# Putting the last four residual-token tiles of a routed MLP behind a run-time branch

## The chip, the cores and the metric

One core of one Trainium2 chip runs the whole program in one launch. Five engines work side by side, each through its own instruction list: PE (matrix products), DVE (vector), ACT (scalar, activation functions), POOL (here mostly the issue of gathers and scatters) and SP (here only the issue of DMAs). Engines wait for each other on semaphores. The metric is the device time of one execution in microseconds (us).

## The reference

An attention without softmax, then a mixture of experts with one expert per token, then a dense MLP, all in float32. Cut to what matters:

```
out  = u * (relu(z z^T / S)^2 v)                 # 8 batches, S = 3072, D = 256
x    = out as 24576 tokens of 256
e    = argmax of the cosine logits of x, per token, over 8 experts
y[t] = gate[t] * (relu(x[t] w1[e]) w2[e])        # hidden width 1024
res  = elu(y w_in) w_out                         # hidden width 2048
```

Which expert a token goes to is known only once the attention is done, so the counts of the experts are numbers on the chip, while the program is fixed.

## The kernel before

The program is unrolled: a list of *steps* is built first (lines 1323 to 1370), and one loop at the end (lines 1555 to 1571) emits for each step its PE work, its DVE and ACT work with a lag of one step, and the second matrix product with a lag of two (LAG). Tasks such as loads and gathers are hung on a step number with `at`. That emission order is the order on every engine: nothing reorders it later.

The steps come in units:

- Attention: 48 chunks of 512 tokens (to 1.9 ms of the run).
- **A**, 41 tiles of 512 tokens that all belong to one expert: 4 steps, `ab_h` and `a_acc`, 96 matmuls of 512 columns.
- **B**, 21 tiles of up to 256 *residual* tokens (what an expert has left after its full tiles): 2 steps, `ab_h` and `b_acc`, 96 matmuls of 256 columns. Its rows are gathered through the id list, and its results are scattered into a dense table `dn` (3584 rows) and their ids into `dnid`.
- **M**, the dense MLP of an A tile: 8 steps of 24 matmuls of 512 columns (`m_h` and `m_acc`).
- **D**, the dense MLP of the 3584 residual tokens in `dn`: 7 tiles of 512, each like an M.

The order is six A with their M, then triples A, B, M as long as there are B tiles, then pairs A, M, then the seven D.

The 21 is the most that the counts can make necessary (`NB`, line 43). A plan computed by DVE (`plan2_ops`, line 857) makes `G`, the number of 256-row tiles of each expert's residue, its running sum `cG`, and `tl`, the last sum less one. A tile with a number above `tl` takes the indices of tile `tl` again, and its scatter indices are raised by 1.0e6, beyond the bound of the scatter:

```
lambda: ts(keep("tl", [128, 1]), K["cG"][:, E - 1:E], -1.0, ALU.add),
lambda: ts(k2("tq"), K["jt"][:, :J], K["tl"], ALU.min),
lambda: tt(k2("ov"), K["jt"][:, :J], h["tq"], ALU.is_gt),
```

Buffers: working tiles come from 45 slots of 4 KB per partition (tag "g"); `pss` and `psa` are PSUM tiles, two each. A matmul that writes a `pss` buffer waits for the engines that last read it.

Of the kernel before, what the change touches and what calls it, by code (L numbers as in the profile page):

```python
# [7 lines left out]
F32 = mybir.dt.float32  # L8
F32R = mybir.dt.float32r
BF16 = mybir.dt.bfloat16  # L10
I32 = mybir.dt.int32
# [17 lines left out]
def attn_moe_mlp(ctx, tc, zT, zK, uT, v, emb, embT, tau, wp, w_in, w_out, out):  # L29
    nc = tc.nc  # L30
    B, DZ, S = zT.shape
    D = uT.shape[1]
# [8 lines left out]
    NA = ceil_div(N - E * 511, 512)  # L41
    NR = N - 512 * NA
    NB = (NR + E * 255) // 256
    ND = NR // 512
    NA1 = 6
    MAXT = 8
    assert D == 256 and DZ == 64 and E == 8 and NR % 512 == 0 and NR <= 14 * 256
# [6 lines left out]
    XW = D + 64  # L54
# [8 lines left out]
    mir = {(b, c, k): dr.tile([128, 2048], F32, name="mir")  # L63
           for b in range(B) for c in range(NC) for k in range(c + 1, NC)}

    def slot(name, dt=F32, shape=(2, 512)):
        return sb.tile([128] + list(shape), dt, name=name, tag="g", bufs=NSLOT)

    def rslot(name):
        return slot(name, F32R)  # L70

    def wide(name, shape):
        return sb.tile([128] + shape, F32, name=name, tag="wide", bufs=NWIDE)

    def t_sm():
        return sb.tile([128, MAXT * E], F32, name="sm", tag="sm", bufs=11)

    def t_ps():
        return ps.tile([128, 2, 512], F32, name="pss", tag="s", bufs=2)

    def t_acc():
        return ps.tile([128, 2, 512], F32, name="psa", tag="acc", bufs=2)

    def const(shape, dt, name):
# [7 lines left out]
    def ts(o, a, s1, op0, s2=None, op1=None):  # L92
        if op1 is None:
            vec.tensor_scalar(out=o, in0=a, scalar1=s1, scalar2=None, op0=op0)
        else:
            vec.tensor_scalar(out=o, in0=a, scalar1=s1, scalar2=s2, op0=op0, op1=op1)
# [37 lines left out]
    def at(n, fn, s=0):  # L134
        tasks[n][s].append(fn)
# [722 lines left out]
    def plan2_ops():  # L858
        NA2 = NA - NA1
        J = NB  # L860
        h = {}

        def start_():
            arena["t"], arena["o"] = [], 0
            tt(keep("c2", [128, E]), K["run"], K["eoff"], ALU.subtract)

        def k3(n):
            h[n] = keep(n + "B", [128, J, E])
            return h[n]

        def k2(n, w=None):
            h[n] = keep(n + "B", [128, J] if w is None else [128, J, w])
            return h[n]

        def dot_(name, src, ind):
            return [lambda: tt(k3("x" + name), h[ind], bj(K[src], J), ALU.mult),
                    lambda: red(k2(name), h["x" + name], ALU.add)]
        ops = [start_] + full_ops("c2", "F2")
        ops += [lambda: tt(K["F2"], K["F2"], K["takena"], ALU.subtract)]
        ops += cum_ops("F2", "cF2") + tile_plan_ops(NA2, "F2", "cF2", "b", "takena")  # L880
        ops += [
            lambda: tt(keep("tk2", [128, E]), K["F2"], K["cF2"], ALU.subtract),
            lambda: ts(K["tk2"], K["tk2"], float(NA2), ALU.add, 0.0, ALU.max),
            lambda: tt(K["tk2"], K["tk2"], K["F2"], ALU.min),
            lambda: tt(K["tk2"], K["tk2"], K["takena"], ALU.add),
            lambda: stt(keep("r", [128, E]), K["tk2"], -512.0, K["c2"], ALU.mult, ALU.add),
            lambda: tt(keep("gt", [128, E, 14]), be_(K["r"], 14),
                       K["mr"].unsqueeze(1).broadcast_to([128, E, 14]), ALU.is_gt),
            lambda: red(keep("G", [128, E]), K["gt"], ALU.add)]
        ops += cum_ops("G", "cG")  # L890
        ops += [
            lambda: ts(keep("tl", [128, 1]), K["cG"][:, E - 1:E], -1.0, ALU.add),
            lambda: ts(k2("tq"), K["jt"][:, :J], K["tl"], ALU.min),
            lambda: tt(k3("cmp"), b2(h["tq"], J, E), bj(K["cG"], J), ALU.is_ge),
            lambda: red(k2("e"), h["cmp"], ALU.add),
            lambda: ts(k2("w"), h["e"], 128.0, ALU.mult, K["pcol"], ALU.add),
            lambda: vec.tensor_copy(keep("wiB", [128, J], I32), h["w"]),
            lambda: onehot(k3("oh"), h["cmp"])]
        ops += dot_("g", "G", "cmp") + dot_("p", "r", "cmp") + dot_("k", "tk2", "oh") + dot_("r", "r", "oh")
        ops += [  # L900
            lambda: tt(h["g"], h["tq"], h["g"], ALU.subtract),
            lambda: stt(h["r"], h["g"], -256.0, h["r"], ALU.mult, ALU.add),
            lambda: ts(h["e"], h["e"], float(N), ALU.mult),
            lambda: stt(h["e"], h["k"], 512.0, h["e"], ALU.mult, ALU.add),
            lambda: stt(h["e"], h["g"], 256.0, h["e"], ALU.mult, ALU.add),
            lambda: stt(h["p"], h["g"], 256.0, h["p"], ALU.mult, ALU.add),
            lambda: ts(k2("cl"), h["r"], -1.0, ALU.add),
            lambda: tt(k2("ixf", 2), tpj(J, 2), b2(h["cl"], J, 2), ALU.min),
            lambda: tt(h["ixf"], h["ixf"], b2(h["e"], J, 2), ALU.add),
            lambda: vec.tensor_copy(keep("ixB", [128, J, 2], I32), h["ixf"]),  # L910
            lambda: tt(k2("ov"), K["jt"][:, :J], h["tq"], ALU.is_gt),
            lambda: tt(k2("od", 2), tpj(J, 2), b2(h["r"], J, 2), ALU.is_ge),
            lambda: tt(h["od"], h["od"], b2(h["ov"], J, 2), ALU.add),
            lambda: ts(h["od"], h["od"], 1.0e6, ALU.mult),
            lambda: tt(h["od"], h["od"], b2(h["p"], J, 2), ALU.add),
            lambda: tt(h["od"], h["od"], tpj(J, 2), ALU.add),
            lambda: vec.tensor_copy(keep("dpB", [128, J, 2], I32), h["od"])]

        return ops + [arena.clear]
# [43 lines left out]
    def rows_ops(key):  # L963
        kind, j = key
        nt = 4 if kind == "A" else 2

        def idx(t):
            if kind == "A":
                return K["ixa"][:, j, t:t + 1] if j < NA1 else K["ixb"][:, j - NA1, t:t + 1]
            return K["ixB"][:, j, t:t + 1]  # L970
        h = {}

        def gi(t):
            def fn():
                if t == 0:
                    IDS[key] = sb.tile([128, 4], I32, name="ids", tag="ids", bufs=8)
                    h["x"] = wide("rows", [4, XW])
                gather(IDS[key][:, t:t + 1], tok[:, :], idx(t), E * N - 1)
            return fn

        def gx(t):
            def fn():
                gather(h["x"][:, t], xr[:, :], IDS[key][:, t:t + 1], N - 1)
            return fn
        row = (j if kind == "A" else NA + j) * 512
        rows = xg[row:row + nt * 128, :]

        def gate(t):
            def fn():
                x = h["x"][:, t]  # L990
                ts(x[:, :D], x[:, :D], x[:, D:D + 1], ALU.mult)
            return fn

        def put():
            sp.dma_start(rows.rearrange("(t p) d -> p t d", p=128), h["x"][:, :nt, :D])

        def get():
            h["t"] = slot("xt", F32, (16, 2, 32))
            for i in range(4):
                sp.dma_start(h["t"][i * 32:(i + 1) * 32, :nt * 4].rearrange("p b a c -> p b (a c)"),  # L1000
                             rows.rearrange("(b r) d -> r b d", r=32)[:, :, i * 64:(i + 1) * 64])
        return [gi(t) for t in range(nt)] + [gx(t) for t in range(nt)], [gate(t) for t in range(nt)], put, get, h
# [40 lines left out]
    def ab_d(key, i):  # L1043
        lo = rslot("lo")
        stt(lo, PS.pop((key, i)), 0.0, f(HL[key, i][0]), ALU.max, ALU.subtract)
        HL[key, i][1] = lo
# [293 lines left out]
        units += [("A", j), ("M", j - 1)]  # L1340
    units += [("M", NA1 - 1)]
    j, t = NA1, 0
    while j < NA and t < NB:
        units += [("A", j), ("B", t), ("M", j)]
        j += 1
        t += 1
    if j < NA:
        units += [("A", j)]
        j += 1
        while j < NA:  # L1350
            units += [("A", j), ("M", j - 1)]
            j += 1
        units += [("M", NA - 1)]
    elif t < NB:
        last = units.pop()
        while t < NB:
            units += [("B", t)]
            t += 1
        units.append(last)
    units += [("D", i) for i in range(ND)]  # L1360
    mf = {"h": m_h, "g": m_g, "d1": m_d, "d2": m_d2, "d3": m_hi, "d4": m_lo, "acc": m_acc}
    lf = dict(mf, h=l_h, acc=l_acc)
# [131 lines left out]
    for un in units:  # L1494
# [47 lines left out]
        if k in "MD" and un != units[-1]:  # L1542
# [4 lines left out]
            at(w + 2, get)  # L1547
            spread(sc, w + 4, w + 6)

    def emit(n, k):  # L1550
        if 0 <= n < len(steps):
            steps[n][0].get(k, none)(*steps[n][1])

    for n in range(len(steps) + LAG):
        emit(n, "h")
        emit(n - 1, "d1")
        one_task(n)
        emit(n - 1, "d2")
        one_task(n)
        emit(n - 1, "d3")  # L1560
        one_task(n)
        emit(n - 1, "d4")
        for fn in pre.pop(n, ()):
            fn()
        emit(n - LAG, "acc")
        emit(n, "g")
        run_tasks(n)
# [42 lines left out]
```

## Time and profile before

| | us |
|---|---|
| median of 3 runs | 5202.31 |
| lowest, highest | 5199.91, 5210.75 |
| profiled execution | 5196.12 |
| its span, first to last instruction | 5194.3 |
| PE busy in it | 5159.3 (99%) |
| DVE busy in it | 4146.7 (80%) |
| ACT busy in it | 3540.4 (68%) |
| POOL busy in it | 1424.0 (27%) |

A matmul's start is recorded and its end is modelled, so how fast PE goes is read from the distance of starts. In the steady state a 512-column matmul starts 0.227 us after the one ahead of it, and a 256-column one 0.120 us.

### The profile page before, as it was taken

What the parts mean: (1) busy time and instruction counts of PE and PEld (TensorE: products, weight loads), DVE (VectorE), ACT (ScalarE), POOL (GpSimd) and SP (SyncE); (2) the same over time, 40 slices, a digit from 0 to 9 for tenths busy, and PEclk for the clock granted to TensorE, in tenths of its full rate; (3) what the DMA queues carried; (4) which work ended last, traced back from release to release, by engine and by line L of the source; (5) the groups of instructions that cost most, each with busy time, mean ns of one, the idle gap of its engine ahead of it and who ended that gap; (6) DMA issues with size and microseconds to landing.
All of it is one profiled execution on the core that took longest, in us unless ns stands there. A gap on an engine that the chain in (4) does not pass through costs nothing. (4 is left out here: it accounts for less than half of the span.)

```text
span 5194.3 us, 67824 instructions
## 1 busy us (share of the span) xinstructions
PE 5159.3 (99%) x23792; PEld 4301.4 (83%) x23792; DVE 4146.7 (80%) x5425; ACT 3540.4 (68%) x4196; POOL 1424.0 (27%) x1207
## 2 busy tenths in 40 slices
PE   9999999999999999999999999999999999999998
PEld 7888888888888878888888888888888888888887
DVE  8888888888888877887777777787787777777887
ACT  8676777767676855676666666666666666666776
POOL 0111111111111133334444444444444333331011
PEclk9999999999999999999999999999999999999999
DMA  7988888797969694323433433434433333231221
GB/s 234 232 214 213 212 199 222 201 223 201 222 183 233 186 233 135 86 75 112 120 107 104 124 102 108 127 102 115 115 105 101 83 84 84 84 82 50 46 48 37
DMA packets 720983, 720.15 MB, mean 139 GB/s; under 512 B 422460, under 2 KB 628543, under 8 KB 705280
## 3 DMA queue, kind: packets, MB, share of 16 engines
q1 hardware_dynamic: 643584, 502.17, 38.4%
q0 software_dynamic: 77056, 213.63, 13.5%
q8 instruction: 188, 3.08, 0.3%
q14 instruction: 155, 1.27, 0.1%
HBM read 450.95 MB, written 254.14 MB: 136 GB/s over the span
## 5 line engine op out<-in xcount | busy, mean ns | idle before, releaser
L111 PE MATMUL psa<-hi,v 128*128 128x512 f32 x4608 | 1143.3, 390 | 0.2 <-DVE hi L510 0.2
L111 PEld LDWEIGHTS psa<-hi,v 128*128 128x128 f32 x4608 | 862.6, 188 | 181.9 <-DVE hi L510 2.2
L111 PE MATMUL pss<-x2h,wi 128*128 128x512 f32 x2624 | 808.7, 389 | 0.0
L111 PE MATMUL psa<-hi,wo 128*128 128x512 f32 x3008 | 743.0, 389 | 0.0
L100 DVE SCALAR_TENSOR_TENSOR y<-e,y 128x1024 f32<-128x1024 f32 x384 | 467.4, 1217 | 301.7 <-ACT e L1164 274.3
L111 PEld LDWEIGHTS psa<-hi,wo 128*128 128x128 f32 x3008 | 564.4, 188 | 117.0
L1110 ACT ACTIVATE e<-pss 128x1024 f32<-128x1024 f32 x376 | 386.4, 1028 | 396.1 <-PE pss L111 355.0
L111 PE MATMUL psa<-lo,v 128*128 128x512 f32 x2304 | 618.0, 390 | 8.1 <-DVE lo L90 7.2
L1036 ACT ACTIVATE hi<-pss 128x1024 fp32r<-128x1024 f32 x206 | 211.9, 1029 | 588.2 <-PE pss L111 556.0
L426 ACT ACTIVATE r<-pss 128x1024 f32<-128x1024 f32 x336 | 344.8, 1026 | 362.9 <-PE pss L111 344.6
L727 POOL DMA_INDIRECT tok<-idt,pi x192 | 236.6, 1233 | 1278.4 <-DMA tok<-idt,pi 771.8
L111 PEld LDWEIGHTS pss<-x2h,wi 128*128 128x128 f32 x2624 | 489.8, 188 | 99.4
L111 PEld LDWEIGHTS psa<-lo,v 128*128 128x128 f32 x2304 | 431.5, 188 | 103.1 <-DVE lo L90 12.0
L111 PE MATMUL pss<-x2l,wi 128*128 128x512 f32 x1312 | 510.4, 389 | 0.0
L90 DVE TENSOR_TENSOR lo<-r,hi 128x1024 fp32r<-128x1024 f32 x336 | 408.4, 1215 | 124.6 <-ACT hi L108 122.3
L90 DVE TENSOR_TENSOR y<-r,y 128x1024 f32<-128x1024 f32 x384 | 470.5, 1225 | 34.6 <-DVE y L100 2.3
L930 POOL DMA_INDIRECT out<-o,ids x192 | 238.5, 1242 | 944.2 <-DMA o<-orow 485.2
L90 DVE TENSOR_TENSOR lo<-y,hi 128x1024 fp32r<-128x1024 f32 x384 | 470.7, 1226 | 20.4
L1164 ACT ACTIVATE e<-e 128x1024 f32<-128x1024 f32 x384 | 407.8, 1062 | 12.2
L1163 ACT ACTIVATE y<-e 128x1024 f32<-128x1024 f32 x384 | 407.2, 1060 | 9.5
L111 PE MATMUL psa<-hi,w 128*128 128x512 f32 x1312 | 404.9, 390 | 0.0
L111 PE MATMUL pss<-xh,w 128*128 128x512 f32 x1312 | 404.3, 389 | 0.3 <-DVE lo L100 0.2
(184 smaller groups left out, 9566.9 us busy)
## 6 DMA issues: line engine op xcount, KB each, us to landing
mir<-mt SPq DMA_DIRECT2D x120, 1024.0 KB
mr<-mir SPq DMA_DIRECT2D x960, 128.0 KB
vs<-v SPq DMA_DIRECT2D x48, 512.0 KB
u<-uT SPq DMA_DIRECT2D x48, 512.0 KB
xr<-xt SPq DMA_DIRECT2D x192, 128.0 KB
x<-xr SPq DMA_DIRECT2D x48, 512.0 KB
orow<-xt SPq DMA_DIRECT2D x188, 128.0 KB
o<-orow SPq DMA_DIRECT2D x47, 512.0 KB
```

Of the source, the lines that this page charges most:

```text
L90: vec.tensor_tensor(out=o, in0=a, in1=b, op=op)
L100: vec.scalar_tensor_tensor(out=o, in0=a, scalar=s, in1=b, op0=op0, op1=op1)
L111: pe.matmul(o, lhsT=l, rhs=r, start=start, stop=stop, skip_group_check=True)
L426: act.activation(out=r, in_=p, func=AF.Relu, scale=1.0 / S)
L727: pool.indirect_dma_start(out=tok[:, :], out_offset=bass.IndirectOffsetOnAxis(ap=h["pi"][:, t:t + 1], axis=0), in_=K["idt"][:, gt:gt + 1], ...
L930: pool.indirect_dma_start(out=dst, out_offset=bass.IndirectOffsetOnAxis(ap=idx, axis=0), in_=src, in_offset=None, bounds_check=bound, oob_ ...
L1036: act.activation(out=hi, in_=p, func=AF.Relu)
L1110: act.activation(out=e, in_=p, func=AF.Relu, scale=-1.0)
L1163: act.activation(out=y, in_=e, func=AF.Tanh, scale=0.5)
L1164: act.activation(out=e, in_=e, func=AF.Exp, scale=-1.0)
```

## The change

The units now hold 17 of the 21 B tiles (`NBS`): there are 17 triples and then pairs. The other four stand, one after the other, in a block between the last M and the first D. At the block every engine reads one number and either goes through the block or jumps over it. The number is `tl`, copied to an integer (`taken_tiles`) in the plan and loaded into a register of each engine three steps ahead of the block; the block is entered if it is at least 17, that is, if more than 17 tiles hold rows. Inside the block, tiles are taken in turn from a small set allotted for it (17 of the "g" slots, both `pss`, one `psa`).

```diff
+    NBS = NB - 4
...
     def slot(name, dt=F32, shape=(2, 512)):
+        if fixed:
...
+            t = again("gr" if dt == F32R else "g")[:, :w]
...
             lambda: ts(keep("tl", [128, 1]), K["cG"][:, E - 1:E], -1.0, ALU.add),
+            lambda: vec.tensor_copy(keep("taken_tiles", [128, 1], I32), K["tl"]),
...
-    while j < NA and t < NB:
+    while t < NBS:
         units += [("A", j), ("B", t), ("M", j)]
...
+    def load_count():
+        count["v"] = nc.values_load(K["taken_tiles"][0:1, 0:1], min_val=0, max_val=NB)
+
+    def rest_tiles():
+        with tc.If(count["v"] >= NBS):
+            mine = {"g": [slot("rest", F32, (1024,)) for _ in range(5)],
+                    "gr": [slot("restr", F32R, (1024,)) for _ in range(12)], "wide": [wide("rows", [4, XW])],
+                    "s": [t_ps() for _ in range(2)], "acc": [t_acc()],
+                    "ids": [sb.tile([128, 4], I32, name="ids", tag="ids", bufs=8)]}
+            fixed.update(mine)
+            for t in range(NBS, NB):
...
+            fixed.clear()
+
+    n_rest = start["D", 0]
+    at(n_rest - 3, load_count)
...
     for n in range(len(steps) + LAG):
+        if n == n_rest:
+            rest_tiles()
         emit(n, "h")
```

On PE, before, the first D tile's matmuls (`pss<-xh,wi`) stand right behind the last M tile's (`psa<-lo,wo`):

```order
L111 MATMUL psa<-lo,wo 128x512 [waits DVE_49]
L111 MATMUL psa<-lo,wo 128x512 x3
L111 MATMUL pss<-xh,wi 128x512 [waits PE_49,Activation_49]
L111 MATMUL pss<-xh,wi 128x512
L111 MATMUL pss<-xl,wi 128x512 [waits DVE_49]
```

Now a compare-and-branch stands between them, then the block (its matmuls read and write `restr`, `pss`, `psa`), and then the end of the block, whose second branch is the way for those that jumped:

```order
L134 MATMUL psa<-lo,wo 128x512 [waits DVE_49]
L134 MATMUL psa<-lo,wo 128x512 x3
L1574 COMPARE_AND_BRANCH
L134 MATMUL pss<-restr 128x256 [waits PE_49,Activation_49]
L134 MATMUL pss<-restr 128x256 [waits DVE_49] x2
...
L1574 UNCONDITIONAL_BRANCH
L1574 UNCONDITIONAL_BRANCH [waits PE_49]
L134 MATMUL pss<-xh,wi 128x512 [waits DVE_49,PE_49,Activation_49]
L134 MATMUL pss<-xh,wi 128x512
L134 MATMUL pss<-xl,wi 128x512
```

The jump waits for PE's own last matmul, and the first D matmul, which waited for PE and ACT, now waits for DVE too.

On DVE, now, the same gate stands behind the `lo` of the last M tile's seventh step, and DVE's last work in the block reads `pss`:

```order
L1203 CAST hi<-y 128x1024 [waits DVE_49]
L113 TENSOR_TENSOR lo<-y,hi 128x1024 [waits DVE_49,PE_49]
L1574 COMPARE_AND_BRANCH
L117 TENSOR_SCALAR rows<-rows 128x256 [waits DMASW2_49]
...
L123 SCALAR_TENSOR_TENSOR restr<-pss,restr 128x1024 [waits Activation_49] x2
L1574 UNCONDITIONAL_BRANCH
L1574 UNCONDITIONAL_BRANCH [waits DVE_49]
L123 SCALAR_TENSOR_TENSOR y<-e,y 128x1024 [waits PE_49,Activation_49]
```

Before, that `lo` and the next `y` stood side by side. ACT has the gate behind the `r` of the last M tile's eighth step, with a jump that waits for ACT's own work.

## Rows read from the trace of the kernel before

**Rows 1.** The page's head and its busy times, with share and instructions.
```profile
span 5194.3 us, 67824 instructions
PE 5159.3 (99%) x23792; PEld 4301.4 (83%) x23792; DVE 4146.7 (80%) x5425; ACT 3540.4 (68%) x4196; POOL 1424.0 (27%) x1207
```

**Rows 2.** Waits of PE: engine tile line <- releaser: us in total, times, longest.
```profile
PE psa L111 <- DVE lo L90: 8.7, 10, 1.7
PE pss L111 <- ACT zk L108: 6.2, 1, 6.2
...
```

**Rows 3.** Windows: stretch, length, busy (instructions) by engine, PEclk, DMA, GB/s.
```profile
3719.30:3796.20 76.90, 76.90 (x386) 65.58 (x385) 59.23 (x68) 49.92 (x60) 33.20 (x29) 1.00 0.39 109
4624.80:4690.10 65.30, 65.30 (x289) 54.08 (x289) 49.84 (x54) 42.60 (x48) 20.50 (x16) 1.00 0.30 83
```

**Rows 4.** Timeline of PE: first matmuls of four A tiles (start, length).
```profile
3796.16 0.61 PE L111 MATMUL pss<-xh,w 128*128 128x512 f32 x2
...
3873.04 0.62 PE L111 MATMUL pss<-xh,w 128*128 128x512 f32 x2
...
4624.84 0.62 PE L111 MATMUL pss<-xh,w 128*128 128x512 f32 x2
...
4690.12 0.61 PE L111 MATMUL pss<-xh,w 128*128 128x512 f32 x2
```

**Rows 5.** Groups of PE by form: the first product of the B tiles.
```profile
L111 PE MATMUL pss<-xb,w 128*128 128x256 f32 x1008 | 127.5, 283 | 0.0
```

**Rows 6.** Windows, POOL's `dn` scatters: behind the first scatter of tiles 16, 17, 20.
```profile
3610.80:3613.10 2.30, 0.98 (x1) 1.00 0.16 57
...
3687.70:3690.00 2.30, 0.96 (x1) 1.00 0.01 0
...
3918.30:3920.60 2.30, 0.98 (x1) 1.00 0.01 0
```

**Rows 7.** Timeline of DVE, PE and ACT where the first D tile begins.
```profile
4857.37 1.23 DVE L90 TENSOR_TENSOR lo<-y,hi 128x1024 fp32r<-128x1024 f32 x1
...
4863.30 1.07 PE L111 MATMUL psa<-lo,wo 128*128 128x512 f32 x4
...
4864.20 0.61 PE L111 MATMUL pss<-xh,wi 128*128 128x512 f32 x2
...
4864.51 1.23 DVE L90 TENSOR_TENSOR lo<-y,hi 128x1024 fp32r<-128x1024 f32 x1
...
4864.80 1.01 ACT L1095 ACTIVATE r<-pss 128x1024 f32<-128x1024 f32 x1
```

**Rows 8.** Timeline of SP and POOL in the last M tile: results out.
```profile
4833.04 1.95 SPq L544 DMA_DIRECT2D orow<-xt  x4
...
4844.93 1.66 POOL L930 DMA_INDIRECT out<-o,ids  x1 [59.32 <-DMA o<-orow]
...
4854.18 1.95 POOL L930 DMA_INDIRECT out<-o,ids  x1 [2.02 <-DMA out<-o,ids]
```

**Rows 9.** DMA queues: packets, MB, share of 16 engines.
```profile
q8 instruction: 188, 3.08, 0.3%
```

**Rows 10.** Timeline of PE: the start at half clock, and its longest later pause.
```profile
8.48 0.63 PE L111 MATMUL pss<-zq,zk 128*128 128x512 f32 x1
...
8.91 0.63 PE L111 MATMUL pss<-zp,zk 128*128 128x512 f32 x1
...
1854.78 1.20 PE L111 MATMUL psa<-lo,v 128*128 128x512 f32 x4 [1.69 <-DVE lo L90]
...
5178.96 0.28 PE L111 MATMUL psa<-wo,lo 128*128 128x256 f32 x1
```

**Rows 11.** Windows with PEclk: around that pause, and behind PE's last matmul.
```profile
1852.60:1855.00 2.40, 0.71 (x4) 0.28 (x3) 2.03 (x6) 1.34 (x3) 2.10 (x2) 1.00 1.18 215
...
5181.40:5194.00 12.60, 0.00 (x0) 0.00 (x0) 0.00 (x0) 0.00 (x0) 0.97 (x1) 0.50 0.06 21
```

More of the change, by code (lines that the diff above doesn't have):

```diff
@@ L64, in attn_moe_mlp, with again @@
            for b in range(B) for c in range(NC) for k in range(c + 1, NC)}
-    def slot(name, dt=F32, shape=(2, 512)):
+    fixed = {}
+    def again(tag):
+        q = fixed[tag]
+        q.append(q.pop(0))
+        return q[-1]
+    def slot(name, dt=F32, shape=(2, 512)):
+        if fixed:
+            w = 1
+            for s_ in shape:
+                w *= s_
+            t = again("gr" if dt == F32R else "g")[:, :w]
+            if len(shape) == 1:
+                return t
+            names = "abcd"[:len(shape)]
+            return t.rearrange("p (%s) -> p %s" % (" ".join(names), " ".join(names)), **dict(zip(names[1:], shape[1:])))
         return sb.tile([128] + list(shape), dt, name=name, tag="g", bufs=NSLOT)
@@ L72, in wide @@
     def wide(name, shape):
+        if fixed:
+            return again("wide")
         return sb.tile([128] + shape, F32, name=name, tag="wide", bufs=NWIDE)
@@ L78, in t_ps @@
     def t_ps():
+        if fixed:
+            return again("s")
         return ps.tile([128, 2, 512], F32, name="pss", tag="s", bufs=2)
     def t_acc():
+        if fixed:
+            return again("acc")
         return ps.tile([128, 2, 512], F32, name="psa", tag="acc", bufs=2)
@@ L975, in fn @@
                 if t == 0:
-                    IDS[key] = sb.tile([128, 4], I32, name="ids", tag="ids", bufs=8)
+                    IDS[key] = again("ids") if fixed else sb.tile([128, 4], I32, name="ids", tag="ids", bufs=8)
                     h["x"] = wide("rows", [4, XW])
@@ L1346, in attn_moe_mlp @@
         t += 1
-    if j < NA:
-        units += [("A", j)]
+    units += [("A", j)]
+    j += 1
+    while j < NA:
+        units += [("A", j), ("M", j - 1)]
         j += 1
[L1350 to L1359, printed above, removed]
+    units += [("M", NA - 1)]
+    assert ND * 512 - (NB - NBS) * 256 >= 5 * 512
     units += [("D", i) for i in range(ND)]
@@ L1548, in attn_moe_mlp @@
             spread(sc, w + 4, w + 6)
+    count = {}
+    def load_count():
[8 more added lines that the diff above has]
+            for t in range(NBS, NB):
+                un = ("B", t)
+                wl, w1, w2 = weight_ops(un)
+                ro, gates, put, get, h = rows_ops(un)
+                tr, hl = xt_ops(un, h, XT, 2)
+                for o in ro + wl + gates + [put] + [o for x in w1 for o in x] + [get] + [o for x in w2 for o in x] + [tr] + hl:
+                    o()
+                for k in range(2):
+                    ab_h(un, k)
+                    ab_d(un, k)
+                for k in range(2):
+                    b_acc(un, k)
+            fixed.clear()
+    n_rest = start["D", 0]
+    at(n_rest - 3, load_count)
     def emit(n, k):
```

## The prediction

> **What bounds the kernel now.** I read the busy times first: PE is busy for 5159.3 of 5194.3 us, 99%, every other engine for 80% or less [rows 1]. A busy PE is not yet a PE at its pace, so the waits of PE came next. There are eight rows of them, 19.6 us together, and the two largest, 8.7 us in ten waits for DVE's `lo` and 6.2 us in one wait, are most of it [rows 2]; asked for the stretch from 2400 to 4863 us alone, which holds the triples and pairs spoken of here, the same view gives no wait at all. The reader is to see in the windows that PE fills them: 76.90 of 76.90 us in a triple A, B, M, and 65.30 of 65.30 in a pair A, M [rows 3], at full clock. So in this part of the program the end moves by what PE's list gets shorter or longer, as long as DVE and ACT keep up.
>
> What a B tile costs PE is then a difference of distances, not a sum of modelled durations. From the A tile at 3796.16 to the next at 3873.04 a triple takes 76.88 us; from 4624.84 to 4690.12 a pair takes 65.28 [rows 4]. A B tile is worth 11.60 us. The check: 96 matmuls of 256 columns (48 of them are the first product, 1008 in 21 tiles [rows 5]) at the 0.120 us between starts make 11.5.
>
> **Is the block entered?** Everything turns on whether more than 17 tiles hold rows. The trace tells it. A tile above `tl` scatters out of bounds, so its `dn` scatter moves nothing. In the 2.30 us behind the first `dn` scatter of tile 16 the DMA engines moved 57 GB/s, which is 131 KB, or 128 rows of 1 KB; behind that of tile 17 and that of tile 20 it is 0 [rows 6]. So tiles 0 to 16 hold rows, 17 to 20 repeat tile 16, `tl` is 16, and 16 >= 17 is false. The reference's own routing of its inputs leaves residues of 458, 457, 129, 86, 379, 114, 428 and 1533 tokens: 2+2+1+1+2+1+2+6 = 17 tiles. The block is jumped over.
>
> **What the change removes.** Four B tiles leave the list: 4 x 11.60 = 46.4 us of PE. The other engines lose their share too (in the windows DVE goes from 59.23 to 49.84 and POOL from 33.20 to 20.50 us [rows 3]), none of which sets the end. Four triples become pairs, a form that already runs without a gap in the trace, so no new wait takes the place of the time saved.
>
> **What it adds.**
>
> One small DVE copy in the plan, of 128x1: between nothing and some 0.2 us, beside PE's work; taken as 0.
>
> A register load on each engine, three steps (16.3 us) ahead of the block. The trace has none. On PE it stands in front of work whose inputs are long there: the `lo` for the matmuls at 4863.30 was done at 4857.37 + 1.23 = 4858.60, 4.7 us earlier [rows 7], so PE's list can be read ahead by about that much. A load dearer than that would show. On DVE and ACT a pause is made up before PE needs the result. I take 0; if the cover is gone, the nearest row for a round trip through memory is the 2.02 us that POOL waited for a DMA [rows 8].
>
> The gate. It costs something, since PE goes through this point now without a gap: at 4863.30 the last four `lo` matmuls, at 4864.20 the first D matmul [rows 7]. Nothing can be gained here. Three things are new. (a) PE's jump waits until its own last matmul is finished: four matmuls take 1.07 us [rows 7], at 0.227 us between starts 0.39 us for the last one, so 0.2 us is lost at least. (b) The first D matmul writes a `pss` buffer that, by the order of the program, was last read inside the block by DVE and ACT. So it waits until DVE and ACT have passed the end of the block, which in a jump they mark only when their own earlier work is finished. In the trace of before, DVE's `lo` at this place ends at 4864.51 + 1.23 = 4865.74 and ACT's `r` at 4864.80 + 1.01 = 4865.81, while PE began D at 4864.20 [rows 7]. PE will stand for 1.6 us. (c) The branch itself, the semaphores of the jump, and the restart of PE's stream. No row shows them. The lower end is the 0.2 of (a), the upper one a round trip like the 2.02 us on each of two engines one behind the other, 4 us [rows 8]. I take 0.6, near the lower end, because the fetch of instructions lies beside the 1.6 us of (b): DVE's and ACT's jumps are short (some 50 instructions), and PE's can be read ahead by the 4.7 us above.
>
> PE's jump goes over 4 x 96 matmuls with their weight loads, 768 instructions, and instructions come in packets of 3.08 MB / 188 = 16.4 KB, which took 0.3% of 16 x 5194.3 us / 188 = 1.3 us each [rows 9]. The Trainium skill speaks against the change here: on the page "Runtime: NRT & Kernel Launch", section "Instruction fetch mechanics", a taken branch whose target is not among the blocks at hand stalls until the target's block has been fetched. By that rule alone the sum would be some 1.3 us less favourable or more; that the fetch is hidden behind the read-ahead is my estimate, and no row of before shows a branch.
>
> POOL and SP must pass the block too, and they do so when all their DMAs have landed. Queued behind are POOL's scatters and SP's transfers of the next tile. POOL's last scatter ahead of it was issued at 4854.18 and took 1.95 [rows 8], 8 us before PE arrives, and SP's are older. Both have passed when ACT and DVE get there, and nothing on PE hangs on them.
>
> After the gate nothing new is late: DVE and ACT restart with the same backlog as PE, and the D tiles run as before.
>
> **Sum.** -46.4 + 1.6 + 0.6 = -44.2 us. Against the profiled execution: 5196.12 - 44.2 = 5151.9, span 5150.1. The median of the three runs, 5202.31, lies 6.2 us above the profiled execution; from it, 5158.1. The forecast is 5158 us, its own range 5154 to 5167, since the runs shown go from 2.4 below to 8.4 above their median.
>
> **Rivals.**
>
> *A dear gate.* The load, the branches and the fetches come one after the other on the engine that is last, and the pause lets PE's clock fall. The trace has one pause of 1.69 us [rows 10] through which the granted clock stayed at 1.00 [rows 11]; behind the last matmul, which began at 5178.96, it had fallen to 0.50 by 5181.4 [rows 10, 11], and the pause forecast here lies between the two. At the start, at half clock, matmuls stood 0.43 us apart (8.48, 8.91) instead of 0.227 [rows 10], so for as long as that lasts about half of the time is lost: 2 us if it lasts 4. With 4 us instead of 0.6, a load that shows (2 us) and the clock (2 us) the change is worth 46.4 - 1.6 - 8 = 36.8: 5165.5. For it: no row shows any of its parts cheap. Against: the slack in rows 7.
>
> *The removed work was cover.* Something that ran beside the four B tiles (gathers of the next A tile, DVE's catching up) would now be waited for, and the time stays. Then 5202 less little: 5195 to 5205. Against it are the pairs, where DVE is busy for 49.84 of 65.30 us and PE has no gap [rows 3].
>
> *The block is entered* (slower). It decides at the eighteenth tile. Then the 46.4 us are back, and the tiles run with nothing beside them: before its first matmul a tile needs ids, rows, a write to DRAM and a read back. The same way out and back takes 4844.93 - 4833.04 = 11.9 us for results [rows 8], and two gathers ahead of it about 2 us each with a wait: some 18 us that PE stands idle at least once and at most four times. So 5202 + 18 + 2 to 5202 + 72 + 2: 5222 to 5276, the middle 5250. Against it is the traffic of rows 6.
>
> *The change does nothing*, because the jump is not taken as written or the four tiles' work is done anyway: this would be the 5202 of before, or the rival above.
>
> **How the numbers follow.** The forecast has 0.74, the dear gate 0.19, the lost cover 0.03, the entered block 0.03, no effect 0.01. What a measurement of this kernel can tell from no change is about 0.2%, 10.4 us. Forecast and dear gate are both faster by more than that, as are a few outcomes of the cover between them: 0.94. Within 0.2%: 0.03. Slower: 0.03. The range has to reach over the dear gate and over the scatter of runs: from 5149 (all of 46.4 us gained, a low median) to 5172 (the dear gate with the median a few us high). Entered block and lost cover stay outside, with 0.07.
>
> **What would show it.** In the profile of the changed kernel: 17 triples at 76.88 us, then pairs at 65.28 without a gap; no matmul of the block's `restr` tiles; 4 x 96 matmuls fewer; exactly one new pause of PE, ahead of the first D matmul, of about 2.2 us, released by ACT or DVE, both of which end their last work ahead of the gate 1.6 us after PE would have begun; D tiles 43.5 us apart as before. Wrong would be: matmuls on `restr` (entered), a pause well over 3 us there or matmuls 0.43 us apart behind it (dear gate), a second pause at the register load (the load is not covered), or gaps in the new pairs (cover).

## The result, and the profile after

The changed kernel takes 5155.55 us (median of 4, 5149.88 to 5161.02) against 5201.11 us (5196.81 to 5210.75): ratio 0.991, 95% interval 0.9891 to 0.9929. A second time, on another occasion, it took 5151.82 us against 5199.99: 0.9904, 0.9887 to 0.992. The forecast was 5158 us.

The page of the kernel after gives PE as busy as before, with 384 matmuls fewer, the four tiles' 4 x 96 [rows 1]:

```profile
span 5159.2 us, 66786 instructions
PE 5117.7 (99%) x23408; PEld 4257.6 (83%) x23408; DVE 4109.3 (80%) x5370; ACT 3511.3 (68%) x4148; POOL 1363.3 (26%) x1159
```

The timeline of PE after (start, length), at the first triple, at two triples and at two pairs, answers to [rows 4]:

```profile
2349.07 0.61 PE L134 MATMUL pss<-xh,w 128*128 128x512 f32 x2
...
3502.27 0.62 PE L134 MATMUL pss<-xh,w 128*128 128x512 f32 x2
...
3579.15 0.62 PE L134 MATMUL pss<-xh,w 128*128 128x512 f32 x2
...
4656.98 0.62 PE L134 MATMUL pss<-xh,w 128*128 128x512 f32 x2
...
4722.26 0.62 PE L134 MATMUL pss<-xh,w 128*128 128x512 f32 x2
```

A triple takes 3579.15 - 3502.27 = 76.88 us and a pair 4722.26 - 4656.98 = 65.28, as before, and the four former triples are now pairs.

The timeline where the first D tile begins, after, answers to [rows 7]:

```profile
4830.16 1.07 PE L134 MATMUL psa<-lo,wo 128*128 128x512 f32 x4
...
4831.37 1.23 DVE L113 TENSOR_TENSOR lo<-y,hi 128x1024 fp32r<-128x1024 f32 x1
...
4831.66 1.00 ACT L1119 ACTIVATE r<-pss 128x1024 f32<-128x1024 f32 x1
...
4832.81 0.70 PE L134 MATMUL pss<-xh,wi 128*128 128x512 f32 x2 [1.58 <-ACTq L1574]
```

PE's last matmul ends at 4831.23. ACT's `r` ends at 4832.66, DVE's `lo` at 4832.60, and 0.15 us behind ACT the first D matmul starts. Against the normal 0.227 us between starts PE lost 1.74 us here (the four `lo` matmuls begin at 4830.16, so the next would have begun at 4831.07). The instructions of the gate on each engine's sequencer, the part that reads its instruction list (count, duration ns, start; PE's sequencer is PEldq in this view), after:

```profile
L1574 SPq COMPARE_BRANCH  x1: 50/50/50, 4808.3 to 4808.3; - x1
L1574 POOLq COMPARE_BRANCH  x1: 45/45/45, 4820.5 to 4820.5; - x1
...
L1574 PEldq COMPARE_BRANCH  x1: 3391/3391/3391, 4827.0 to 4827.0; - x1
L1574 ACTq COMPARE_BRANCH  x1: 50/50/50, 4830.7 to 4830.7; - x1
L1574 PEldq EVENT_SEMAPHORE  x1: 51/51/51, 4831.3 to 4831.3; - x1
L1574 DVEq COMPARE_BRANCH  x1: 72/72/72, 4831.4 to 4831.4; - x1
L1574 DVEq EVENT_SEMAPHORE  x1: 21/21/21, 4832.6 to 4832.6; - x1
L1574 ACTq EVENT_SEMAPHORE  x1: 17/17/17, 4832.7 to 4832.7; - x1
```

PE's branch takes 3.39 us, but its sequencer came to it at 4827.0, 4.2 us before PE's array had finished; it was through at 4830.4. On the other engines a branch takes 0.05 to 0.07 us. SP and POOL passed long before. The register loads, by the same view of their line, are 0.46 to 0.55 us each:

```profile
L1571 PEldq TENSOR_LOAD <-taken_tiles x1: 491/491/491, 4816.1 to 4816.1; - x1
L1571 DVEq TENSOR_LOAD <-taken_tiles x1: 546/546/546, 4818.9 to 4818.9; - x1
L1571 ACTq TENSOR_LOAD <-taken_tiles x1: 462/462/462, 4820.3 to 4820.3; - x1
```

The two profiled executions side by side, by stages cut at PE's matmul starts:

| stage | before | after | difference |
|---|---|---|---|
| start to the first triple | 2335.44 | 2349.07 | +13.63 |
| first triple to first D matmul | 2528.76 | 2483.74 | -45.02 |
| first D matmul to last matmul | 314.75 | 314.88 | +0.13 |
| last matmul to the end | 15.36 | 11.51 | -3.85 |
| span | 5194.3 | 5159.2 | -35.1 |

The second line is what the prediction was about. The first and the last were not in it, and the experiments had to tell what they are.

### The profile page after: what moved, and what is told of

It is laid out like the page before. It is cut to its first block, busy times and chain, and to the rows that moved or that the text cites. A ratio compares the mean times of both kernels' runs of the same rounds, so it can differ in the third digit from the quotient of the medians.

```text
span 5159.2 us, 66786 instructions
## 1 busy us (share of the span) xinstructions
PE 5117.7 (99%) x23408; PEld 4257.6 (83%) x23408; DVE 4109.3 (80%) x5370; ACT 3511.3 (68%) x4148; POOL 1363.3 (26%) x1159
## 3 DMA queue, kind: packets, MB, share of 16 engines
q0 software_dynamic: 73472, 203.91, 13.1%
```

## The experiments

**The changed kernel again.**

> The changed kernel once more. Theory of the prediction (PE's list is 46.4 us shorter, one gate pause of 1.7 us): the pause ahead of the first D tile is again 1.7 us, triples 76.88 and pairs 65.28 us, and the time is 0.991 of the kernel before. In the first profile of the changed kernel PE also stood longer in the attention stage, and the first A tile behind the sixth M began at 2349 us against 2335 before. If that belongs to the execution, this profile shows another value between 2330 and 2350; the rival, that the change causes it (other waits in that stage), wants 2349 again, within 2 us, with pauses at the same places.

5151.82 us (5150.65 to 5155.14), ratio 0.9904 (0.9887 to 0.992). The pause is 1.58 us again, and from the first triple to the first D matmul it is 2483.7 us again. The first triple began at 2343.2 us, not at 2349: PE stood at three of the same places, 237, 474 and 967 us, but for a shorter time.

**The gate alone.** All 21 tiles stay in the triples, with the block behind them besides:

```diff
-    while t < NBS:
+    while t < NB:
```

> All 21 B tiles stay in the triples, and the block with its gate stands ahead of the D tiles besides, never entered. Theory: the gate's price alone, 1.7 us on PE, so 5201 + 2 = 5203 us, no change that can be measured, and one pause of 1.6 us ahead of the first D matmul with ACT or its sequencer as releaser. Rival (the gate or the longer program costs more than its pause, in the attention stage too): 5210 us or more. Rival (the gate gives back time elsewhere): 5195 or less.

5201.08 us against 5199.99, ratio 1.0002 (0.9992 to 1.0011): no change that a timing tells. Its timeline of PE has the same pause:

```profile
4866.37 0.70 PE L134 MATMUL pss<-xh,wi 128*128 128x512 f32 x2 [1.58 <-ACTq L1574]
```

From the first triple to the first D matmul it takes 2530.74 us against 2528.76, 2.0 us more: the 1.74 us, and 0.24 at another place (a wait for a weight behind the last triple). In this stage the gate does nothing else. From the last matmul to the end it is 15.86 us against 15.36; POOL's drain there is as long as before (10.177 us), and what the half microsecond is was not found.

**The removal alone.** No block and no load:

```diff
-        if n == n_rest:
-            rest_tiles()
...
-    at(n_rest - 3, load_count)
```

> The four tiles are left out of the units and there is no block and no load: tiles 17 to 20 are never computed. Theory: 46.8 us less than before, 5154 us, no pause ahead of the first D tile, from the first triple to the first D matmul 2482.0 us. Rival (the four tiles' work was cover and part of the 46.4 us comes back as a wait): over 5165 us with new gaps in the pairs. Rival (the gate costs much more than its pause): 5145 us or less, over 5 us better than the changed kernel.

5154.08 us, ratio 0.9907 (0.989 to 0.9923). There is no pause ahead of D, but the stage takes 2483.06 us and not the 2482.0 expected. Among the waits of PE is one that the changed kernel does not have:

```profile
PE pss L134 <- DVE w L113: 0.6, 1, 0.6
```

It stands behind the last triple. The stretch from there over an A tile and the first pair A, M takes 88.10 us; without a gap it is 21.76 + 65.28 = 87.04, and that is what the changed kernel takes. So 1.06 of the 46.4 us came back as a wait in this version, for a reason that was not looked into, and none of them in the changed kernel. The rival that wants over 5165 us is out, and the gate's price lies within the scatter of the timings.

**The block entered.**

```diff
-        with tc.If(count["v"] >= NBS):
+        with tc.If(count["v"] >= NBS - 1):
```

> The condition is one lower (at least 16), so the block is entered, and tiles 17 to 20 do the work of tile 16 again with their scatters out of bounds. This prices the slower rival of the prediction: 5222 to 5276 us, 5250 in the middle, that is 66 to 120 us in the block (18 to 72 us of PE standing beside 46.4 us of matmuls). If the block's tiles overlap each other well (gathers of the next tile under the matmuls of this one): under 75 us in the block; if each waits for the one before to its end: over 110 us.

5298.29 us (one execution), 98 more than before, beyond the range for this rival. From the first triple to the first D matmul it takes 2630.05 us; without the block it would be 2483.74 - 1.74 = 2482.0, so the block takes 148 us, against 66 to 120 expected. The waits of PE, then the timeline at the first and second tile:

```profile
PE pss L134 <- ACT restr L131: 91.2, 4, 25.8
```

```profile
4833.80 7.93 PE L134 MATMUL pss<-restr 128*128 128x256 f32 x48 [15.39 <-ACT restr L131]
...
4873.24 8.58 PE L134 MATMUL pss<-restr 128*128 128x256 f32 x48 [25.76 <-ACT restr L131]
```

PE stands for 15.4 us ahead of the first tile and for 25.8 ahead of the second, 91.2 us in four pauses. What is in those 25.8 us is read from POOL, ACT, DVE and SP (timelines of the same kernel):

```profile
4811.80 1.76 POOL L949 DMA_INDIRECT ids<-tok,ixB  x1 [0.30 <-issue]
...
4848.45 1.01 POOL L954 DMA_INDIRECT dn<-rest,dpB  x1 [22.56 <-ACT rest L131]
...
4852.33 1.05 POOL L949 DMA_INDIRECT ids<-tok,ixB  x1 [0.31 <-issue]
...
4862.42 1.00 POOL L949 DMA_INDIRECT rest<-wp,wiB  x1 [0.30 <-issue]
```

```profile
4847.58 0.60 ACT L131 ACTIVATE rest<-psa 128x512 f32<-128x512 f32 x1 [4.79 <-PE psa L134]
4862.83 0.63 ACT L131 ACTIVATE restr<-rest 128x512 fp32r<-128x512 f32 x1 [14.65 <-DMA rest<-wp,wiB]
...
4869.89 1.15 ACT L131 ACTIVATE restr<-rest 128x512 fp32r<-128x512 f32 x2 [0.70 <-DMA rest<-wp,wiB]
4872.56 0.63 ACT L131 ACTIVATE restr<-rest 128x512 fp32r<-128x512 f32 x1 [1.52 <-DVE rest L1032]
```

```profile
4870.55 1.29 DVE L113 TENSOR_TENSOR restr<-rest,restr 128x512 fp32r<-128x512 f32 x2 [0.34 <-ACT restr L131]
4871.76 0.70 DVE L1032 STREAM_TRANSPOSE rest<-rest 128x512 f32<-128x512 f32 x1
```

```profile
4867.17 1.85 SPq L1024 DMA_DIRECT2D rest<-xg  x4
```

From its first gather of ids to its first matmul the first tile takes 4833.80 - 4811.80 = 22.0 us, the second 4873.24 - 4852.33 = 20.9. The first tile's gathers began 6.6 us before PE ran out of work; the second's began 4.8 us after it, since on POOL's list the scatters of the first tile's results stand ahead of them. Within a tile the four weight gathers stand behind the two for ids and the two for rows. The last weights are there at 4869.89, and DVE goes straight from their conversion to the transpose of the rows, without a wait for the rows' read-back (issued from 4867.17 on). So the weights ended last, though the rows cannot have been far ahead of them. And the clock falls in the pauses (windows of the same kernel; PEclk, the share of the full clock granted to PE, is the number behind the five engines):

```profile
4820.71:4837.78 17.07, 3.98 (x17) 3.76 (x18) 6.70 (x11) 5.22 (x9) 4.02 (x4) 0.50 0.51 154
4838.00:4851.00 13.00, 9.48 (x80) 9.28 (x78) 2.45 (x2) 2.65 (x3) 1.98 (x2) 1.00 0.01 1
4851.43:4878.70 27.27, 5.46 (x24) 5.24 (x25) 7.10 (x12) 5.15 (x9) 10.03 (x10) 0.50 0.35 109
```

So the first product of each tile runs in part at half clock: from its first matmul to the second product's it takes 7.8 to 8.8 us in the four tiles, against 48 x 0.120 = 5.8, together 10.1 us more. With 91.2 us of standing and 46.4 of matmuls that makes 147.7 of the 148 us.

**The block without `pss`.**

```diff
-                    "s": [t_ps() for _ in range(2)], "acc": [t_acc()],
+                    "acc": [t_acc()],
...
+            mine["s"] = list(mine["acc"])
             fixed.update(mine)
```

> The block works in one psa buffer alone and takes no pss, so the first D matmul no longer has to wait until DVE and ACT have passed the block. Theory (the pause is the wait for ACT's and DVE's last work through pss): the pause of 1.6 us goes and what is left is PE's own end, 0.2 to 0.5 us between the last psa matmul's end and the first D matmul; the time is 1.2 us below the changed kernel, which no timing tells apart, so 5151 us. Rival (the pause is the branch itself, its 3.4 us on PE's sequencer): the pause stays at 1.5 us or more.

5148.6 us (5147.48 to 5151.76), ratio 0.9903 (0.9887 to 0.992). Timeline of PE, then its sequencer:

```profile
4817.92 1.07 PE L134 MATMUL psa<-lo,wo 128*128 128x512 f32 x4
4819.28 0.70 PE L134 MATMUL pss<-xh,wi 128*128 128x512 f32 x2 [0.30 <-PEq L1574]
```

```profile
L1574 PEldq COMPARE_BRANCH  x1: 3911/3911/3911, 4814.8 to 4814.8; - x1
...
L1574 PEldq EVENT_SEMAPHORE  x1: 51/51/51, 4819.0 to 4819.0; - x1
```

The pause goes from 1.58 to 0.30 us, and its releaser is now PE's own sequencer. The branch is as long as ever. So the pause was the wait for ACT and DVE through `pss`, and the branch is not in it. Of the versions run that still hold all the tiles, this one is the best by its trace, 1.3 us better than the changed kernel in this stage; the timings do not tell the two apart.

**The load directly ahead of the gate.**

```diff
-    at(n_rest - 3, load_count)
+    at(n_rest - 1, load_count)
```

> Each engine loads the number directly ahead of the gate, not three steps earlier. The load takes 0.46 to 0.55 us on the engines' sequencers in the profile of the changed kernel. Theory (the sequencers run ahead, and the end of ACT's work sets the gate): pause unchanged, 1.5 to 1.8 us. Rival (the load counts on the engine that is last): pause 2.1 to 2.2 us.

The pause is 1.58 us (one execution, 5151.55 us). PE's branch began at 4818.2, took 3.58 us and was through at 4821.8, just when the array had finished: the read-ahead was used up, but nothing was lost.

**One tile in the block.**

```diff
-            for t in range(NBS, NB):
+            for t in range(NBS, NBS + 1):
```

> The block holds one tile and not four (tiles 18 to 20 are left out), so PE's jump goes over a quarter of the instructions. Theory (the 3.4 us of PE's compare-and-branch are the fetch of a target that is not at hand): the branch takes 0.2 us or less. Rival (any taken branch of PE costs 3.4 us, or it is the wait for PE's own work): 3.3 us or more again. The pause stays at 1.5 to 1.8 us by either, since ACT sets it.

The pause is 1.71 us (one execution, 5151.33 us), and PE's branch is short, by the view of its line:

```profile
L1574 PEldq COMPARE_BRANCH  x1: 232/232/232, 4817.3 to 4817.3; - x1
```

A jump over 192 instructions takes 0.23 us, one over 768 takes 3.4 to 3.9, and the engines' own work was the same. So it is the distance and not a wait for PE's own work. That it is the fetch of the target is borne out by the DMA traffic. In the changed kernel the only packet in the 3.4 us of the branch (4827.0 to 4830.4) is one of 16 KB on the instruction queue; with one tile no packet falls in the 3.4 us from the branch's start (4817.3 to 4820.7). The two lines, in this order:

```profile
q8 instruction: 1, 0.02, 1.7%
```
```profile
DMA packets 0, 0.00 MB, mean 0 GB/s; under 512 B 0, under 2 KB 0, under 8 KB 0
```

In each of the six traces with a long branch such a packet starts 1.0 to 1.5 us behind the branch's start and lands within it, after some 1 us; in the two with a short branch none does. What fills the rest of the 3.4 us is not recorded.

**The kernel before again.**

> The kernel before once more, for the attention stage. Its first A tile behind the sixth M began at 2335.4 us in the first profile; the changed kernel's at 2349.1 and 2343.2, the same program with the block entered at 2336.2, without the block at 2343.0. If the difference belongs to the execution, before shows a value between 2333 and 2350, and its time against the first profile's moves with it; if it belongs to the program, 2335.4 again within 1 us. One more draw near 2335 leaves it open.

The first triple began at 2341.0 us, not at 2335.4 (5201.69 us, one execution). From there to the first D matmul it is 2528.78 us, as before within 0.02.

**19, 24 and 20 tiles ahead of the D tiles.** `NBS = NB - 2`; then `NB` raised by 3 in the kernel before; then `NBS = NB - 1`.

> 19 B tiles in the triples and 2 in the block, not entered. On PE: first triple to first D matmul 2483.7 + 2 x 11.6 = 2506.9 us. It is also for what stands behind PE's last matmul: 15.3 us in the kernels that executed 21 tiles (1128 gathers and scatters of POOL), 11.5 us in those with 17 (1080), with a last drain of POOL of 10.2 and 6.3 us. Theory (the drain grows with the number of POOL's DMAs, 0.082 us each): 1104 of them, a drain of 8.2 us. Rival (it depends on something else, such as where the last ones fall): 6.3 or 10.2 us again, or anything else.

> The kernel before with three more B tiles, which repeat the last one and scatter out of bounds. On PE: 2528.8 + 3 x 11.6 = 2563.6 us from the first triple to the first D matmul, so some 35 us more than before, 5236 us. POOL's gathers and scatters are 1164: by the theory of a drain that grows with their number 13.1 us, by the rival any other length.

> 20 B tiles in the triples and one in the block, not entered: 2483.7 + 3 x 11.6 = 2518.5 us from the first triple to the first D matmul; POOL's gathers and scatters are 1116, its last drain 9.2 us if it grows with their number; 6.3 or 10.2 if not. The jump goes over one tile, so PE's compare-and-branch takes 0.2 us as with one tile before.

The stage takes 2507.2, 2564.0 and 2519.1 us: 11.7 to 11.9 us per tile between 17, 19, 20 and from 21 to 24, above the 11.60. The difference lies in one place. In each of these traces, and in those of the kernel before and after, every triple takes 76.88 us and every pair behind the first 65.28; only the stretch behind the last triple (87.04 us without a gap) varies: 87.04, 87.31 and 87.57 us with 17, 19 and 20 tiles, 87.41 and 87.84 with 21 and 24 in the kernel before. So a tile costs 11.60 us, and up to 0.8 us is lost once, in waits there. Times of one execution each: 5181.77, 5236.61 and 5189.5 us. POOL's last drain (count; shortest, median and longest ns; first and last start) in the kernel before, after, and with 20, 19 and 24 tiles:

```profile
L1605 POOLq DRAIN  x3: 51/102/10177, 5183.4 to 5194.0; - x3
```
```profile
L1654 POOLq DRAIN  x3: 51/113/6257, 5152.1 to 5158.9; - x3
```
```profile
L1654 POOLq DRAIN  x3: 51/113/9197, 5177.7 to 5187.4; - x3
```
```profile
L1654 POOLq DRAIN  x3: 51/113/8217, 5170.9 to 5179.7; - x3
```
```profile
L1605 POOLq DRAIN  x3: 51/102/4463, 5229.6 to 5234.6; - x3
```

With 1080, 1104, 1116 and 1128 gathers and scatters executed it lasts 6.257, 8.217, 9.197 and 10.177 us: 0.0817 us for each, to the nanosecond. The other runs agree: it is within 0.006 us of 6.257 in all six traces with 1080, and of 10.177 in all four with 1128, whether the last four tiles run in the triples or in the block. With 1164 it is not 13.1 but 4.463, so the growth does not go on, and where it breaks off was not found. My theory held up to 1128 and fell at 1164; the rival of a fixed pair of values is out. That it is the gathers and scatters that count is still a reading: they come 12 to a B tile, and no run changes them alone.

## Why the prediction was right

**The block is not entered: right.** No matmul on a `restr` tile is in the trace, and 384 matmuls are missing. The rows that said so were the DMA traffic of the scatters [rows 6].

**46.4 us of PE leave: right.** The stage from the first triple to the first D matmul went from 2528.76 to 2483.74 us. With the 1.74 us of the gate taken out that is 46.8: 4 x 11.60, and 0.4 from the waits behind the last triple, which took 0.37 us before (87.41 against 87.04) and nothing now. Only 0.07 us of that is idle time by the profile, too little for a row in the view that showed the prediction no wait in this stage. That PE's list alone set the time, with no cover lost, is shown by 17, 19, 20, 21 and 24 tiles, whose triples and pairs are equal to 0.01 us.

**The gate: right in mechanism, its last term too dear.** Part (b), 1.6 us until ACT's and DVE's work ahead of the gate ends, came as read from [rows 7], and the block without `pss` shows that it is the cause. Part (c), put at 0.6 us for branch, semaphores and restart, measured 0.15 from ACT's end to PE's start. The pause was forecast at 2.2 us and cost 1.74. The load cost nothing, and neither did its place.

**The fetch: hidden as estimated, but longer.** The branch takes 3.4 us, not the 1.3 us of one packet [rows 9], and lay wholly in front of the end of PE's own work. The Trainium skill, "Runtime: NRT & Kernel Launch", section "Instruction fetch mechanics", says that a taken branch to a target not at hand stalls for a fetch; the traces agree (3.39 us over two or four tiles, 0.23 and 0.39 over one). What it left open here is whether PE pays for it, and PE did not, since its sequencer arrived 4.2 us early. With the load directly ahead of the gate none of that was left.

**What the prediction missed.** It said that the D tiles run as before, and had no term for the end behind them. The D tiles do; the end behind PE's last matmul got 3.85 us shorter, because POOL's last drain got shorter by 3.92 us, with 48 gathers and scatters fewer (48 x 0.0817 = 3.92). The program's own gain is thus 45.0 + 3.85 - 0.1 = 48.7 us, where 44.2 was forecast. The medians give 45.6 and 48.2. That the first median, 5155.55 us, lies so near to 5158 is in part luck: the gain that was not foreseen is of the size of the scatter of the runs. The second, 5151.82, lies below the forecast's own range, which began at 5154.

**The attention stage.** The 13.6 us that the first profile lost ahead of the first triple are not the change's, as far as thirteen traces tell. The kernel before, twice and with three tiles more, reached the first triple at 2335.4, 2341.0 and 2346.0 us, 2340.8 in the mean; the changed kernel and its variants reached it, in ten traces, at 2335.6 to 2349.1 us, 2340.7 in the mean. The same list of instructions, apart from the constant compared, gave 2349.1, 2343.2 and, with the block entered, 2336.2. The spread of the totals, some 10 us in either kernel, is about that of these values. What makes a given execution slow there was not found; in the profiles PE waits for ACT, which waits for data to land. In the slowest one a pause of 2.0 us at 237 us was followed by a stretch at half clock, in the windows of the kernel after:

```profile
239.75:243.16 3.41, 3.41 (x10) 2.64 (x9) 3.12 (x4) 3.38 (x6) 0.00 (x0) 0.50 0.99 286
...
4831.20:4832.80 1.60, 0.03 (x1) 0.03 (x1) 1.30 (x2) 1.47 (x2) 0.00 (x0) 1.00 0.06 15
```

The gate's own pause left the clock at 1.00, so the dear gate of the rivals did not come. Its price for a lost clock rested on the start of the program, where only the distance of the matmuls speaks for half clock; the entered block shows it with the granted clock beside it, 0.50, and 2.0 to 3.1 us lost per tile.

**The slower rival was priced too low.** 5222 to 5276 us were given for an entered block, and it is 5298. The step that failed is the 18 us of standing per tile, worked out from one way out and back through memory [rows 8]. From the first gather to the first matmul it is 19.5 to 22.0 us, since the weight gathers queue on POOL behind the ids and rows of the same tile. The first tile had 6.6 us of that beside PE's last work ahead of the block; each later one has some 5 us on top, for the scatters of the tile before. So PE stood for 91.2 us, where the sum had 72 at most. The 10.1 us of matmuls at half clock, which the sum lacked, come on top.

## What to carry to other kernels

In a stage where one engine has no gap, price removed work by the distance between equal points with and without it, and check that the form without it already runs gapless elsewhere in the trace. A run-time branch that is jumped over costs not its instructions but the meeting it forces: look at which buffers the skipped block would have touched last, and by which engines, since the first instruction behind it waits until those have passed; give the block buffers of its own that the critical engine does not need next. And price the way through the block as well: here an entered block cost 98 us (one execution) against the 46 saved, and since all its four tiles then run, one tile too many is enough for it.

## What the runs showed of the hardware

- A compare-and-branch: 0.05 to 0.07 us on SP, POOL, ACT and DVE over some tens of instructions; on PE 0.23 and 0.39 us over one tile (192 matmuls and weight loads), 3.39 us over two tiles, 3.37 to 3.91 over four, when taken; 0.09 and 0.19 us for the two branches of the entered block. In the long branches, and in none of the short ones, an instruction packet of 16 KB lands.
- A register load from on-chip memory took 0.46 to 0.55 us of the sequencer on every engine, and PE's array felt nothing of it.
- POOL's last drain: 0.0817 us more for each gather or scatter executed, from 1080 (6.257 us) to 1128 of them, then a smaller value again (4.463 us at 1164). An unforeseen 3.9 us of the gain came from it.
- PE's granted clock fell to 0.50 in the pauses of 15 to 26 us of the entered block and stayed at 1.00 through the gate's 1.58 us.
